# Joint grams of two block sizes, and one fixed order for three engines, in an RWKV-6 attention followed by an MLP mixer

## Chip, cores and metric

The kernel runs on one core of one Trainium2 chip. The metric is the device time of one execution in microseconds, from runs of the same program; the median is compared.

The engines are called by the names of the profile: PE (TensorE, the matrix unit), PEld (its weight loads), DVE (VectorE), ACT (ScalarE), POOL (GpSimd) and SP (SyncE, which here only issues DMAs).

## The reference

Two parts follow each other: a recurrent attention with a decay per channel, and a mixer over tokens and channels.

```python
B, H, S, D = 4, 8, 768, 48
for t in range(S):                      # attention, state is (B, H, D, D)
    cur = einsum('bhd,bhe->bhde', u * k[t], v[t])
    y[t] = einsum('bhd,bhde->bhe', r[t], state + cur)
    state = w[t][..., None] * state + einsum('bhd,bhe->bhde', k[t], v[t])
x = y as (B, S, H * D)                  # 384 channels
h = relu(x^T @ w_tok1) @ w_tok2         # tokens: 768 -> 256 -> 768
u = x + h^T
out = u + relu(u @ w_ch1) @ w_ch2       # channels: 384 -> 1536 -> 384
```

All arithmetic is in fp32. The mixer's weights arrive as 64-bit floats and are turned into fp32 by bit operations on VectorE.

## The kernel before

**Attention without a loop over tokens.** The 768 tokens of a batch are cut into three *units* of 256 tokens; there are twelve units, 0 to 11, and unit i belongs to batch i // 3. A unit holds two groups c of 128 tokens, and each of these two chunks of 64. Within a chunk the product of r and k with all decays between two tokens is built as a triangle of weights `at` (per head 64 by 64), and the outputs are `at` times v. Between chunks a state is carried.

The triangle is built by block doubling, in levels l = 0 to 5 with blocks of b = 2^l tokens. At a level, every right block of a pair of neighbours meets its left block: `gram(l)` multiplies k with the r of the right blocks on PE, `pick(l)` copies the wanted squares out of PSUM into `at` (through a mask with copy_predicated on DVE for levels 1 to 3, with four plain copies on ACT for level 4), and `join(l)` multiplies the decay of the neighbouring block into r and k on DVE, in place, so that the next level finds them relative to the bounds of a block twice as wide. `join(l)` changes what `gram(l)` reads, so it waits for it, and `gram(l+1)` waits for `join(l)`. Level 5 is `block(5)`: a gram with 32 weight columns, a join, and four copies on ACT. `begin` does the join of level 0.

[...] The heads have 48 channels, so these products use four tiles of the array, 64 rows by 64 columns each: `fours` issues one product to each of the four in turn. An fp32 product is two instructions on PE.

Units from `NEAR` = 6 on take the diagonal and level 0 from `nearest`: row sums on DVE of r times k for a token and its neighbour, loaded with tokens on partitions by `load_near` into tiles `kp` and `rp`, and then `place`, which puts them into `at`.

After its levels a unit goes through `post`: `tokens` transposes k, `carry` multiplies it with v for the state, `update` works the state on through four chunks on DVE, `before` multiplies r with the state of each chunk, and `within` adds `at` times v to it and copies the result to the mixer's input x on ACT.

**Mixer.** `mixing(bt)` gives lists of pieces for a batch: `hidden` (tokens in, 12 products), `back` and `turn` (tokens out and transposes), `up` (36 pieces, three pieces of 256 tokens by 12 blocks of hidden channels, with the result z taken out by ACT), and `quarters`: the last product by Strassen's seven half-size products p1 to p7 in Winograd's form, for which DVE makes four sums of z (`begin`: s1, s2, s4 and the new a21), and takes each product out of PSUM by an addition into the output o. Only the first piece of batch 0 uses the plain product (`down`).

**Order.** `woven` merges lists of pieces: every piece has a weight, and each list is spread evenly over the whole by weight. `emit` issues them in that order; a scheduler at build time may then move an instruction ahead of others on its engine. `strict` chains the instructions of PE and DVE one to the next, so that their order is the one written; before the change it is used only for the first three units. `beside(i, ...)` gives the pieces of unit i's post together with the levels of unit i + 1; `one` and `both` put the products of two pieces directly behind each other on PE.

The program runs as: units 0 to 2; then mixing 0 woven with units 3 to 5; mixing 1 with units 6 to 8; mixing 2 with units 9 to 11; mixing 3 alone.

**Buffers.** PSUM has two buffers of two banks for grams, transposes of k and (in batches 1 and 2) transposes of x (`ps_g`), one of two banks for state and outputs (`ps_a`), and two of one bank for the mixer's products (`ps_m`). The SBUF tiles named `rp` have two buffers, `kp` has one.

Of the kernel before, what the change touches and what calls it, by code (L numbers as in the profile page):

```python
# [10 lines left out]
f32 = mybir.dt.float32  # L11
bf16 = mybir.dt.bfloat16
u8 = mybir.dt.uint8
# [6 lines left out]
DM = H * D  # L20
T = 64
# [28 lines left out]
def emit(pieces):  # L50
    for _, f in pieces:
        f()
# [3 lines left out]
def rwkv6_then_mixer(  # L56
# [42 lines left out]
    def strict(*fs):  # L99

        for f in fs:
            done = len(block.instructions)
            f()
            for ins in block.instructions[done:]:
                if ins.engine in (pe.engine, dve.engine):
                    tc.add_manual_dep(ins, in_turn[ins.engine], no_sync, reason="order of issue")
                    in_turn[ins.engine] = ins.name

# [136 lines left out]
    def levels(i):  # L245
# [7 lines left out]
        def begin():  # L253
            decay = apool.tile([128, COLS // 2], f32, name="decay")
            L["w"] = apool.tile([128, UC, A, 2], f32, name="w_chunk", bufs=4)
            pool.memset(L["w"], 0.0)
            products.extend([w_, decay, w_[:, :COLS // 4], decay[:, :COLS // 8], w_[:, :COLS // 16],
                             decay[:, :COLS // 32], L["w"].rearrange("p c a j -> p (c a j)")])
            if i >= NEAR:
                join(0, products[0], products[1])  # L260
# [89 lines left out]
        def block(l):  # L350
            gram(l)
            join(l, products[l], products[l + 1])
            pick(l)

        L["steps"] = begin, gram0, pick0, gram, pick, lambda l: join(l, products[l], products[l + 1])
        pieces = [(0.1, begin)] + ([(1.6, first_block)] if i < NEAR else [])
        for l in range(1, LEVELS):
            pieces.append((1.2, lambda l=l: block(l)))
        return pieces

    def load_near(i):
        if i >= NU:
            return
        L = near_by[i] = [apool.tile([128, COLS], f32, name="kp", bufs=1)]
        for c in range(UC):
            t = apool.tile([128, COLS], f32, name="rp")
            sp.dma_start(t[:, :2 * DM].rearrange("p (two e) -> p two e", two=2), near[i - NEAR, c, :, :2, :])
            sp.dma_start(L[0][:, ts(c, DM)], near[i - NEAR, c, :, 2, :])
            L.append(t)

    def nearest(i):

        if not NEAR <= i < NU:
            return [(0.0, lambda: None)] * 2 + [(0.0, begin_near if i == NEAR - 1 else lambda: None)]
        sums = []

        def row(c):
            k, t = near_by[i][0][:, ts(c, DM)], near_by[i][1 + c]
            rr = t[:, :2 * DM].rearrange("p (two e) -> p two e", two=2)
            if c == 0:  # L380
                sums.append(apool.tile([128, UC, 2 * H], f32, name="sums"))
            dve.tensor_mul(rr, rr, k.unsqueeze(1).to_broadcast([128, 2, DM]))
            dve.tensor_mul(rr[:, 0], rr[:, 0], u_rows)
# [15 lines left out]


        return [(0.3, lambda c=c: late(newest(dve), dve, lambda: row(c))) for c in range(UC)] + [
            (0.2, lambda: (place(), load_near(i + 1)))]

    near_by = {}

    def begin_near():

        def parities():
# [3 lines left out]
        late(newest(dve), dve, parities)  # L412
        late(newest(sp), sp, lambda: sp.dma_start(u_rows, u_all))
        load_near(NEAR)

    def post(i):
        bt, half = divmod(i, UB)
# [23 lines left out]
                                      vt[ts(j, T), c, ts(2 * a + q, D)], start=True, stop=True)  # L441

        def update():
            L = live[i]
            kv = L.pop("kv")
            for c in range(UC):
                for j in range(2):
                    g = 2 * (half * UC + c) + j
                    if g == 2 * C - 1:
                        continue  # L450
                    new = apool.tile([128, A, D], f32, name="state", bufs=6)
                    got = kv[:, j, ds(c * A * D, A * D)].rearrange("p (a e) -> p a e", a=A)
                    if g == 0:
                        dve.tensor_copy(new, got)
                    else:
                        dve.tensor_mul(new, state[bt, g], L["w"][:, c, :, j].unsqueeze(2).to_broadcast([128, A, D]))
                        dve.tensor_add(new, new, got)  # L457
                    state[bt, g + 1] = new

# [24 lines left out]
        def within():  # L484
# [9 lines left out]
            for n in range(2):  # L494
                act.copy(x[ts(n, P), 1], got[ts(1 - n, P), 1])

        return [(1.0, tokens), (1.1, carry), (0.1, update), (1.1, before), (1.1, within),
                (0.01, lambda: load_rkw(i + 3)), (0.01, lambda: load_v(i + 3))]

# [19 lines left out]
    def mixing(bt):  # L519
# [51 lines left out]
        def quarters(s):  # L571
# [54 lines left out]
                dve.tensor_add(o[:, 0, HM:], o[:, 0, HM:], product(s4, w22))  # L626
                store(0)

            return [(0.01, begin)] + [(1.96, p) for p in (p1, p4, p2, p5, p6, p7, p3)]
# [11 lines left out]
    def beside(i, after, ahead):  # L641

        tokens, carry, update, before, within, *loads = after
        begin, *rest = ahead
        row0, row1, place = nearest(i + 1)
# [10 lines left out]
        return [(1.0, begin[1]), tokens, one(carry, rest[0]), update, one(before, rest[1]), one(within, rest[2]),  # L656
                *loads, *rest[3:], row0, row1, place]


    hiddens, turned, ups, downs = mixing(0)  # L660
# [8 lines left out]
    for steps in to_tok[:2]:  # L669
        steps[0]()  # L670
    (tok0, car0, upd0, bef0, wit0, *loads0), (tok1, car1, upd1, bef1, wit1, *loads1), (tok2, car2, upd2, bef2, wit2, *loads2) = (
        [f for _, f in post(i)] for i in range(3))
# [13 lines left out]
    for bt in range(B):  # L686
# [8 lines left out]
            pieces = downs[0][-4:] + [(0.01, weight_difference)] + downs[1] + ups[2] + downs[2]  # L695
        else:
            hiddens, pieces, ups, downs = mixing(bt)
            pieces = [(3.9, lambda h=h: emit(h)) for h in hiddens] + pieces
            for s in range(S // SEG):
                pieces += ups[s] + downs[s]  # L700
        n = (bt + 1) * UB
        if n < NU:
            att = []
            if bt == 0:

                begin, first, *rest = levels(n)
                att = [begin, (first[0], lambda f=first[1]: late(in_turn[dve.engine], dve, lambda: late(
                    in_turn[pe.engine], pe, f)))] + [(c, lambda f=f: late(converted, dve, f)) for c, f in rest]
            for i in range(n, n + UB):
                att += beside(i, post(i), levels(i + 1)) if i + 1 < NU else post(i)  # L710
            emit(woven(att, pieces))
        else:
            emit(pieces)

# [34 lines left out]
```

## Time and profile before

| what | us |
|---|---|
| median of 7 runs | 603.58 |
| lowest and highest | 602.91, 604.96 |
| the profiled execution, its own time | 603.58 |
| its span, first to last instruction | 601.9 |
| busy in the span: PE, PEld, DVE, ACT | 570.7, 487.5, 361.1, 177.5 |
| units 0 to 2 and first part of mixing 0 | 0 to 139.5 |
| mixing 0 with units 3 to 5 | 139.5 to 229 |
| mixing 1 with units 6 to 8 | 229 to 364 |
| mixing 2 with units 9 to 11 | 364 to 493 |
| mixing 3 | 493 to 601.9 |

In a row of the profile's groups, the line of the kernel is followed by engine, operation, output and inputs, shapes and count; behind the bar stand the busy time, the mean duration of one, and the idle time of the engine just before these instructions, with what ended it. A row of the timeline gives start and length of a stretch of equal instructions; matmuls overlap in the array, so what a stretch costs is read from its start to the start of the next. The granted clock of TensorE was full from 139.5 us on.

### The profile page before, as it was taken

The numbers are of one execution on the slowest core, as the hardware profiler recorded it, in microseconds if no ns is written. First come the engines' busy times: TensorE is split into PE (matmuls) and PEld (weight loads), VectorE is DVE, ScalarE is ACT, GpSimd is POOL, SyncE is SP. The second block draws the span as 40 slices with busy tenths as digits, with TensorE's granted clock in tenths as the row PEclk, the third lists the DMA queues.
The fourth block names the chain that finished last, engine by engine and source line by source line (L and its number), as shares of the span: only waits on it lengthen the run. The fifth ranks groups of instructions, "written<-read, shape, count | busy, mean of one in ns | idle before, by whom it ended". The sixth has DMA issues, their size and how long they took to land.

```text
span 601.9 us, 18874 instructions
## 1 busy us (share of the span) xinstructions
PE 570.7 (95%) x8596; PEld 487.5 (81%) x8596; DVE 361.1 (60%) x599; ACT 177.5 (29%) x428; POOL 7.2 (1%) x32
## 2 busy tenths in 40 slices
PE   2786999999999999999999999999999999999997
PEld 2776668866888886789989896789898986898987
DVE  5789699999775867666457366528446422040403
ACT  6154444422433313241141231231313312302020
POOL 4000000000000000000000000000000000000000
PEclk9997599999999999999999999999999999999999
DMA  8534555620334225141124113001200000000000
GB/s 331 204 83 152 162 171 177 211 70 19 91 105 111 69 82 158 30 132 29 53 57 132 28 28 106 2 2 35 74 2 28 2 27 0 1 19 8 27 2 27
DMA packets 22976, 45.85 MB, mean 76 GB/s; under 512 B 2512, under 2 KB 14928, under 8 KB 22896
## 3 DMA queue, kind: packets, MB, share of 16 engines
q1 hardware_dynamic: 22752, 44.64, 23.7%
q8 instruction: 67, 1.10, 0.8%
q14 instruction: 13, 0.11, 0.1%
q10 hardware_dynamic: 144, 0.00, 0.0%
HBM read 39.91 MB, written 4.72 MB: 74 GB/s over the span
## 4 chain that ended last, share of the span: by engine, by line
PE 81%; DVE 11%; issue 3%; DMA 2%; ACT 2%; SPq 0%; DVEq 0%; ACTq 0%
PE z_ps L554 26%; PE q_ps L588 24%; PE gram L307 7%; PE h_ps L527 6%; PE h_ps L534 4%; PE kv_ps L440 2%; PE y_ps L476 2%; PE y_ps L489 2%; DVE rk L341 2%; PE h_ps L564 2%; PE gram L430 2%; DVE at L323 1%; PE xT_ps L546 1%; PE gram L301 1%; DVE scratch L218 1%
## 5 line engine op out<-in xcount | busy, mean ns | idle before, releaser
L554 PE MATMUL z_ps<-xT,wch 128*128 128x256 f32 x864 | 195.6, 382 | 0.9 <-ACT z L556 0.9
L554 PEld LDWEIGHTS z_ps<-xT,wch 128*128 128x128 f32 x864 | 161.0, 190 | 22.8 <-ACT z L556 1.8
L556 ACT ACTIVATE z<-z_ps 128x256 f32<-128x256 f32 x144 | 55.1, 383 | 171.1 <-PE z_ps L554 158.2
L588 PE MATMUL q_ps<-wch,z 128*128 128x192 f32 x528 | 94.6, 329 | 0.0
L588 PEld LDWEIGHTS q_ps<-wch,z 128*128 128x128 f32 x528 | 86.1, 190 | 1.4
L588 PE MATMUL q_ps<-scratch,z 128*128 128x192 f32 x396 | 70.0, 328 | 0.0
L307 PE MATMUL gram<-rk 48*64 48x32 f32 x3072 | 62.7, 234 | 5.5 <-issue 2.3
L307 PEld LDWEIGHTS gram<-rk 48*64 48x64 f32 x3072 | 58.5, 153 | 11.1 <-issue 5.1
L341 DVE TENSOR_TENSOR rk<-rk,decay 112x1024 f32<-112x1024 f32 x36 | 44.0, 1223 | 36.7 <-PE gram L307 26.4
L588 PEld LDWEIGHTS q_ps<-scratch,z 128*128 128x128 f32 x396 | 64.5, 190 | 0.4
L341 DVE TENSOR_TENSOR rk<-rk,w 112x1024 f32<-112x1024 f32 x36 | 43.9, 1224 | 27.7 <-PE gram L307 22.0
L580 DVE TENSOR_TENSOR z<-z 128x768 f32<-128x768 f32 x11 | 10.5, 957 | 65.4 <-ACT z L556 65.4
L527 PE MATMUL h_ps<-x,wtok 128*128 128x384 f32 x96 | 35.9, 521 | 0.0
L534 PE MATMUL h_ps<-h,wtok 128*128 128x384 f32 x96 | 35.3, 492 | 0.0
L323 DVE COPY_PREDICATED at<-mask,gram 128x512 f32<-128x512 uint8 x36 | 32.3, 898 | 0.0
L457 DVE TENSOR_TENSOR state<-state,kv_ps 128x192 f32<-128x192 f32 x40 | 14.3, 356 | 24.6 <-PE kv_ps L440 23.8
L331 ACT COPY at<-gram 16x256 f32<-16x256 f32 x48 | 17.5, 364 | 33.6 <-PE gram L307 32.4
L536 DVE TENSOR_TENSOR x<-x,h_ps 128x384 f32<-128x384 f32 x24 | 13.3, 555 | 23.2 <-PE h_ps L534 23.1
L527 PEld LDWEIGHTS h_ps<-x,wtok 128*128 128x128 f32 x96 | 18.5, 201 | 10.4 <-issue 0.6
L534 PEld LDWEIGHTS h_ps<-h,wtok 128*128 128x128 f32 x96 | 16.5, 190 | 9.5 <-ACT h L529 2.6
L431 ACT COPY kT<-gram 128x512 f32<-128x512 f32 x24 | 14.1, 586 | 28.2 <-PE gram L430 28.1
L318 ACT COPY at<-gram 32x256 f32<-32x256 f32 x48 | 17.4, 364 | 14.4 <-PE gram L301 13.9
(84 smaller groups left out, 517.4 us busy)
## 6 DMA issues: line engine op xcount, KB each, us to landing
rk<-in_rkw_dram SPq DMA_DIRECT2D x36, 192.0 KB, 3.3
x<-in_w_ch_dram SPq DMA_DIRECT2D x10, 512.0 KB, 4.4
vt<-in_v_dram SPq DMA_DIRECT2D x12, 384.0 KB, 4.2
out_dram<-o SPq DMA_DIRECT2D x24, 192.0 KB, 1.9
rp<-in_near_dram SPq DMA_DIRECT2D x12, 384.0 KB, 3.6
scratch<-in_w_ch_dram SPq DMA_DIRECT2D x8, 512.0 KB, 4.1
w<-in_rkw_dram SPq DMA_DIRECT2D x18, 192.0 KB, 3.4
rk<-in_rkw_dram SPq DMA_DIRECT2D x6, 512.0 KB, 7.4
```

The source lines that it names most:

```text
L307: fours(lambda q, j, rows, cols: pe.matmul(g[cols, q, ts(ca, 32)], k_[rows, ds(ca * 128 + j * T, T)], right[rows, ts(2 * ca + j, 32 // b), ...
L318: act.copy(at[p:p + b, :, ts(c, A), b:], g[ds(p + c * b, b)])
L323: dve.copy_predicated(out=dst, data=g.rearrange("p q (m b) -> p q m b", b=b), mask=masks[l].rearrange("p x t -> p (x t)").rearrange("p (m ...
L331: act.copy(at[p:p + b, :, :, n * 2 * b + b:(n + 1) * 2 * b], g[p:p + b, :, :, ts(n, b)])
L341: dve.tensor_mul(halves, halves, by)
L431: act.copy(L["kT"][:, c], ps)
L457: dve.tensor_add(new, new, got)
L527: pe.matmul(sums[i], wtok1[:, c, ts(i, 128)], xs[bt][:, c, :], start=(c == 0), stop=(c == C - 1))
L534: pe.matmul(ps, wtok2[:, i, ts(c, 128)], h1[:, i, :], start=(i == 0), stop=(i == DTOK // 128 - 1))
L554: pe.matmul(ps, wch1[:, m, ts(jt, 128)], xT[:, m, ts(s, SEG)], start=(m == 0), stop=(m == DM // 128 - 1))
L556: act.activation(zs[s][:, jt, :], ps, AF.Relu)
L588: pe.matmul(ps, a[:, j, :], b[:, j, :], start=(j == 0), stop=(j == HJ - 1))
```

## The change

For units 6 to 11, the levels 1 and 2, and 3 and 4, are taken in one go. The block of four neighbours (quarters of b tokens) has six pairs. `spread` and `copies` write, for each group of 128 tokens, six blocks of r for every four (three of them with the decays of the quarters between multiplied in, on DVE, and three as copies on ACT) into a tile of the name `rp`. `gram4` multiplies k with them: 96 columns for every chunk instead of 32 in each of two levels. `pick4` copies the squares out with three copy_predicated for each group of tokens. `join_k` and `join_r` then multiply k and r by the decays of the block of four; `join_r` takes r's from the tile that spread filled. Level 5 stays. The masks for pick4 are made once in `begin_near`.

```diff
+        def spread(l, c):
...
+            dve.tensor_mul(y[:, :, 1:5:3], of[:, :, 2:4], by[:, :, 1:3].unsqueeze(3).to_broadcast([ROWS, G, 2, b]))
+            dve.tensor_mul(y[:, :, 2], y[:, :, 4], by[:, :, 1].unsqueeze(2).to_broadcast([ROWS, G, b]))
+        def copies(l):
...
+                act.copy(y[:, :, 0:4:3], r[:, ts(c, G), 1:3])
+                act.copy(y[:, :, 5], r[:, ts(c, G), 3])
+        def gram4(l):
+            for c in range(UC):
+                g = L["g", c] = ps_g.tile([128, 2, 512], f32, name="gram")
+                for a in range(A):
+                    fours(lambda q, j, rows, cols: pe.matmul(
+                        g[cols, q, ts(a, 96)], k_[rows, ds((c * A + a) * 128 + j * T, T)],
+                        L["far", c][rows, ts(2 * a + j, 96)], start=True, stop=True))
+        def join_k(l):
...
+            dve.tensor_mul(w[:, :, 2], w[:, :, 2], w[:, :, 3])
+            dve.tensor_mul(w[:, :, 1], w[:, :, 1], w[:, :, 2])
+            dve.tensor_mul(k[:, :, :3], k[:, :, :3], w[:, :, 1:].unsqueeze(3).to_broadcast([ROWS, UC * G, 3, b]))
+        def join_r(l):
...
+                dve.tensor_mul(r[:, ts(c, G), 1:].rearrange("p g q b -> p g (q b)"), y,
+                               w[:, ts(c, G), 0].unsqueeze(2).to_broadcast([ROWS, G, 3 * b]))
+            dve.tensor_mul(products[l + 2][:ROWS], w[:, :, 0], w[:, :, 1])
+        def pick4(l, c):
...
+            for q, first in enumerate((0, 3, 5)):
+                n = (3 - q) * b
+                dve.copy_predicated(out=to[:, :, :, (q + 1) * b:], data=got[:, :, :, first * b:first * b + n],
+                                    mask=masks4[l][:, q].unsqueeze(1).unsqueeze(3).to_broadcast([128, 2, A * 16 // b, n]))
```

`beside` writes a new order for the units 5 to 10. The row sums of a unit (`nearest`), which came at the end of the stretch before, now open its own stretch, in seven pieces; `update` is cut in two, and `load_near` for the next unit follows the second `join_r`. The three places where `both` puts products together are carry with the first joint gram, before with the second, and within with level 5. The weights of each unit's pieces are scaled to a sum of 12.

```diff
+        pieces = [*nearest(i), (0.3, tokens[1]), (1.9, begin[1]), far0, far1, (1.0, copies[1]), visit(carry, gram), join_k, join_r, loads[2],
+                  later0, pick0, loads[3], later1, copies_, pick1, visit(before, gram_), join_k_, join_r_, (0.01, lambda: load_near(i + 1)),
+                  pick0_, pick1_, visit(within, last), *loads[:2]]
+        total = sum(c for c, _ in pieces)
+        return [(c * 12 / total, f) for c, f in pieces]
```

Here `far` and `later` are spread for l = 1 and l = 3, a trailing underscore stands for l = 3, and loads[2] and loads[3] are the halves of update.

From mixing 1 to the end of mixing 2, `strict` now fixes the order, on ACT too. In the mixings 1 to 3 the four sums of `quarters` stand between the products, the products have weights of their own, and `hidden`, `back` and `turn` have smaller weights; `hidden` is emitted product by product.

```diff
-                if ins.engine in (pe.engine, dve.engine):
+                if ins.engine in in_turn:
...
+            return [(1.6, p1), (0.01, lambda: dve.tensor_add(s1, a21, a22)), (0.65, p4),
+                    (0.01, lambda: dve.tensor_sub(s2, s1, a11)), (0.65, p2), (0.01, lambda: dve.tensor_sub(a21, a11, a21)),
+                    (0.45, p5), (0.01, lambda: dve.tensor_sub(s4, a12, s2)), (0.3, p6), (1.0, p7), (1.6, p3)]
...
-            pieces = [(3.9, lambda h=h: emit(h)) for h in hiddens] + pieces
+            pieces = [(c * 0.5, f) for h in hiddens for c, f in h] + [(c * 0.3, f) for c, f in pieces]
...
-            emit(woven(att, pieces))
+            if bt == 0:
+                emit(woven(att, pieces))
+            else:
+                if bt == 1:
+                    in_turn = {e.engine: newest(e) for e in (pe, dve, act)}
+                strict(*(f for _, f in woven(att, pieces)))
```

More of the change, by code (lines that the diff above doesn't have):

```diff
@@ L259, in begin @@
             if i >= NEAR:
+                products[3], products[5] = w_[:, :COLS // 8], decay[:, :COLS // 32]
                 join(0, products[0], products[1])
@@ L353, in block, with fourths @@
             pick(l)
+        def fourths(l):
+            b = 1 << l
+            return (products[l].rearrange("p (g q) -> p g q", q=4)[:ROWS],
+                    *(t.rearrange("p (g q b) -> p g q b", q=4, b=b)[:ROWS] for t in (k_, r_)), COLS // (4 * b) // UC)
+        def spread(l, c):
+            b = 1 << l
+            w, _, r, G = fourths(l)
+            t = L["far", c] = apool.tile([128, COLS], f32, name="rp")
+            y = t[:, :COLS // UC * 3 // 2].rearrange("p (g s b) -> p g s b", s=6, b=b)[:ROWS]
+            of, by = r[:, ts(c, G)], w[:, ts(c, G)]
+            dve.tensor_mul(y[:, :, 1:5:3], of[:, :, 2:4], by[:, :, 1:3].unsqueeze(3).to_broadcast([ROWS, G, 2, b]))
+            dve.tensor_mul(y[:, :, 2], y[:, :, 4], by[:, :, 1].unsqueeze(2).to_broadcast([ROWS, G, b]))
@@ new lines, in copies @@
+        def copies(l):
+            b = 1 << l
+            _, _, r, G = fourths(l)
+            for c in range(UC):
+                y = L["far", c][:, :COLS // UC * 3 // 2].rearrange("p (g s b) -> p g s b", s=6, b=b)[:ROWS]
+                act.copy(y[:, :, 0:4:3], r[:, ts(c, G), 1:3])
+                act.copy(y[:, :, 5], r[:, ts(c, G), 3])
+        def gram4(l):
+            for c in range(UC):
+                g = L["g", c] = ps_g.tile([128, 2, 512], f32, name="gram")
[3 more added lines that the diff above has]
+                        L["far", c][rows, ts(2 * a + j, 96)], start=True, stop=True))
@@ new lines, in join_k @@
+        def join_k(l):
+            b = 1 << l
+            w, k, r, G = fourths(l)
+            dve.tensor_mul(w[:, :, 2], w[:, :, 2], w[:, :, 3])
+            dve.tensor_mul(w[:, :, 1], w[:, :, 1], w[:, :, 2])
+            dve.tensor_mul(k[:, :, :3], k[:, :, :3], w[:, :, 1:].unsqueeze(3).to_broadcast([ROWS, UC * G, 3, b]))
+        def join_r(l):
+            b = 1 << l
+            w, k, r, G = fourths(l)
+            for c in range(UC):
+                y = L.pop(("far", c))[:, :COLS // UC * 3 // 2].rearrange("p (g s b) -> p g (s b)", s=6, b=b)[:ROWS, :, :3 * b]
+                dve.tensor_mul(r[:, ts(c, G), 1:].rearrange("p g q b -> p g (q b)"), y,
+                               w[:, ts(c, G), 0].unsqueeze(2).to_broadcast([ROWS, G, 3 * b]))
+            dve.tensor_mul(products[l + 2][:ROWS], w[:, :, 0], w[:, :, 1])
@@ new lines, in pick4 @@
+        def pick4(l, c):
+            b = 1 << l
+            to = at_c[:, :, c].rearrange("p q a (m n) -> p q (a m) n", n=4 * b)
+            got = L.pop(("g", c))[:, :, :A * 96].rearrange("p q (m n) -> p q m n", n=6 * b)
+            for q, first in enumerate((0, 3, 5)):
+                n = (3 - q) * b
+                dve.copy_predicated(out=to[:, :, :, (q + 1) * b:], data=got[:, :, :, first * b:first * b + n],
+                                    mask=masks4[l][:, q].unsqueeze(1).unsqueeze(3).to_broadcast([128, 2, A * 16 // b, n]))
@@ L355, in levels @@
         L["steps"] = begin, gram0, pick0, gram, pick, lambda l: join(l, products[l], products[l + 1])
         pieces = [(0.1, begin)] + ([(1.6, first_block)] if i < NEAR else [])
+        if i >= NEAR:
+            return pieces + [(c, lambda f=f, a=a: f(*a)) for l in (1, 3) for c, f, a in (
+                (0.7, spread, (l, 0)), (0.7, spread, (l, 1)), (0.01, copies, (l,)), (0.3, gram4, (l,)), (1.7, join_k, (l,)),
+                (1.5, join_r, (l,)), (1.5, pick4, (l, 0)), (1.5, pick4, (l, 1)))] + [(1.4, lambda: block(5))]
@@ L361, in load_near @@
     def load_near(i):
-        if i >= NU:
-            return
         L = near_by[i] = [apool.tile([128, COLS], f32, name="kp", bufs=1)]
@@ L373, in nearest, with row @@
         if not NEAR <= i < NU:
-            return [(0.0, lambda: None)] * 2 + [(0.0, begin_near if i == NEAR - 1 else lambda: None)]
+            return []
         sums = []
-        def row(c):
+        def row(c, step):
             k, t = near_by[i][0][:, ts(c, DM)], near_by[i][1 + c]
             rr = t[:, :2 * DM].rearrange("p (two e) -> p two e", two=2)
[L380 to L383, printed above, removed]
+            if step == 0:
+                if c == 0:
+                    sums.append(apool.tile([128, UC, 2 * H], f32, name="sums"))
+                dve.tensor_mul(rr, rr, k.unsqueeze(1).to_broadcast([128, 2, DM]))
+                return
+            if step == 1:
+                dve.tensor_mul(rr[:, 0], rr[:, 0], u_rows)
+                return
             dve.tensor_reduce(out=sums[0][:, c], in_=t[:, :2 * DM].rearrange("p (h e) -> p h e", e=D),
@@ L398, in place, with quarters, masks @@
                 mask=masks[0].rearrange("p x (m two) -> p x m two", two=2).to_broadcast([128, 2 * UC * A, T // 2, 2]))
-        return [(0.3, lambda c=c: late(newest(dve), dve, lambda: row(c))) for c in range(UC)] + [
-            (0.2, lambda: (place(), load_near(i + 1)))]
+        return [(x, lambda c=c, n=n: late(newest(dve), dve, lambda: row(c, n)))
+                for c in range(UC) for n, x in enumerate((1.0, 0.6, 1.0))] + [(2.0, place)]
     near_by = {}
+    masks4 = {l: const.tile([128, 3, A * 16 >> l], u8, name=f"mask4_{l}") for l in (1, 3)}
     def begin_near():
+        def quarters(l, m):
+            b = 1 << l
+            n = 16 // b
+            pool.memset(m, 1.0)
+            for q in range(3):
+                for base, by in ((-q * b, 1), (q * b + b - 1, -1)):
+                    pool.affine_select(out=m[:, q], in_=m[:, q], compare_op=ALU.is_ge, fill=0.0, base=base,
+                                       pattern=[[-by * 4 * b, 2 * n]], channel_multiplier=by)
+            for j in range(2):
+                dve.tensor_copy(masks4[l][ts(j, T)].rearrange("p q (a n) -> p q a n", a=A),
+                                m[ts(j, T), :, ts(j, n)].unsqueeze(2).to_broadcast([T, 3, A, n]))
+        def masks():
+            t = apool.tile([128, COLS], f32, name="rp")
+            for l in masks4:
+                quarters(l, t[:, ts(l // 2, 48)].rearrange("p (q n) -> p q n", q=3)[:, :, :32 >> l])
         def parities():
@@ L410, in parities @@
             dve.tensor_scalar(odd, odd, -1.0, 1.0, op0=ALU.mult, op1=ALU.add)
-        late(newest(dve), dve, parities)
+        late(newest(dve), dve, lambda: (parities(), masks()))
         late(newest(sp), sp, lambda: sp.dma_start(u_rows, u_all))
-        load_near(NEAR)
     def post(i):
@@ L443, in update, with update_c @@
         def update():
+            for c in range(UC):
+                update_c(c)
+        def update_c(c):
             L = live[i]
[L445 to L458, printed above, removed]
+            kv = L["kv"] if c == 0 else L.pop("kv")
+            for j in range(2):
+                g = 2 * (half * UC + c) + j
+                if g == 2 * C - 1:
+                    continue
+                new = apool.tile([128, A, D], f32, name="state", bufs=6)
+                got = kv[:, j, ds(c * A * D, A * D)].rearrange("p (a e) -> p a e", a=A)
+                if g == 0:
+                    dve.tensor_copy(new, got)
+                else:
+                    dve.tensor_mul(new, state[bt, g], L["w"][:, c, :, j].unsqueeze(2).to_broadcast([128, A, D]))
+                    dve.tensor_add(new, new, got)
+                state[bt, g + 1] = new
         pairs = ((0, 0), (1, 0), (1, 1), (0, 1))
@@ L497, in post @@
         return [(1.0, tokens), (1.1, carry), (0.1, update), (1.1, before), (1.1, within),
-                (0.01, lambda: load_rkw(i + 3)), (0.01, lambda: load_v(i + 3))]
+                (0.01, lambda: load_rkw(i + 3)), (0.01, lambda: load_v(i + 3)),
+                *((1.4, lambda c=c: update_c(c)) for c in range(UC))]
     halves = [mpool.tile([128, NJ * SEG], f32, name=f"z{i}", bufs=1) for i in range(2)]
@@ L627, in p3 @@
                 store(0)
-            return [(0.01, begin)] + [(1.96, p) for p in (p1, p4, p2, p5, p6, p7, p3)]
+            if bt == 0:
+                return [(0.01, begin)] + [(1.96, p) for p in (p1, p4, p2, p5, p6, p7, p3)]
+            return [(1.6, p1), (0.01, lambda: dve.tensor_add(s1, a21, a22)), (0.65, p4),
+                    (0.01, lambda: dve.tensor_sub(s2, s1, a11)), (0.65, p2), (0.01, lambda: dve.tensor_sub(a21, a11, a21)),
+                    (0.45, p5), (0.01, lambda: dve.tensor_sub(s4, a12, s2)), (0.3, p6), (1.0, p7), (1.6, p3)]
         hiddens = [[(0.65, lambda i=i, c=c: hidden(i, c)) for c in range(C)] for i in range(DTOK // 128)]
@@ L644, in beside @@
         begin, *rest = ahead
-        row0, row1, place = nearest(i + 1)
         def both(f, g):
@@ L653, in one, with visit @@
             return (sum(c for c, _ in pieces), lambda: both(*(f for _, f in pieces)))
-        return [(1.0, begin[1]), tokens, one(carry, rest[0]), update, one(before, rest[1]), one(within, rest[2]),
-                *loads, *rest[3:], row0, row1, place]
+        if i + 1 < NEAR:
+            return [(1.0, begin[1]), tokens, one(carry, rest[0]), update, one(before, rest[1]), one(within, rest[2]),
+                    *loads[:2], *rest[3:], *([(0.0, begin_near)] if i == NEAR - 2 else [])]
+        far0, far1, copies, gram, join_k, join_r, pick0, pick1 = rest[:8]
+        later0, later1, copies_, gram_, join_k_, join_r_, pick0_, pick1_, last = rest[8:]
+        def visit(f, g):
+            return (0.3, lambda: both(f[1], g[1]))
+        pieces = [*nearest(i), (0.3, tokens[1]), (1.9, begin[1]), far0, far1, (1.0, copies[1]), visit(carry, gram), join_k, join_r, loads[2],
[3 more added lines that the diff above has]
+        return [(c * 12 / total, f) for c, f in pieces]
     hiddens, turned, ups, downs = mixing(0)
@@ L671, in rwkv6_then_mixer @@
     (tok0, car0, upd0, bef0, wit0, *loads0), (tok1, car1, upd1, bef1, wit1, *loads1), (tok2, car2, upd2, bef2, wit2, *loads2) = (
-        [f for _, f in post(i)] for i in range(3))
+        [f for _, f in post(i)[:7]] for i in range(3))
     levels(2)
@@ L709, in rwkv6_then_mixer @@
             for i in range(n, n + UB):
-                att += beside(i, post(i), levels(i + 1)) if i + 1 < NU else post(i)
-            emit(woven(att, pieces))
+                att += beside(i, post(i), levels(i + 1)) if i + 1 < NU else nearest(i) + post(i)[:7]
+            if bt == 0:
+                emit(woven(att, pieces))
+            else:
+                if bt == 1:
+                    in_turn = {e.engine: newest(e) for e in (pe, dve, act)}
+                strict(*(f for _, f in woven(att, pieces)))
         else:
```

## Prediction

> **What bounds the kernel now.** First the page's table of engines and its 40 slices, to find the engine that never rests:
>
> ```profile
> PE 570.7 (95%) x8596; PEld 487.5 (81%) x8596; DVE 361.1 (60%) x599; ACT 177.5 (29%) x428; POOL 7.2 (1%) x32
> PE   2786999999999999999999999999999999999997
> DVE  5789699999775867666457366528446422040403
> ```
>
> TensorE (PE) is full from the fifth slice on; VectorE (DVE) has holes. Next the stage windows: start to the first attention woven with mixing (0 to 139.5), the rest of that weave (to 229), mixing 1 with attention (to 364), mixing 2 with attention (to 500), mixing 3 alone:
>
> ```profile
> 139.50:229.00 89.50, 86.59 (x2294) 75.46 (x2294) 66.17 (x114) 29.55 (x77) 0.33 (x3) 1.00 0.29 82
> 229.00:364.00 135.00, 134.67 (x2065) 116.94 (x2064) 85.37 (x150) 36.70 (x92) 0.22 (x2) 1.00 0.24 72
> 364.00:500.00 136.00, 135.94 (x1764) 115.79 (x1763) 66.69 (x123) 33.03 (x82) 0.00 (x0) 1.00 0.10 30
> ```
>
> After span and colon: length, then busy time (and count) of PE, PEld, DVE, ACT, POOL. In mixings 1 and 2 PE is idle for 0.4 us of 271. So two things only can move the end here: PE work taken out, and PE waits put in. There are no waits to win.
>
> What PE work costs is read from its timeline, from start to start (matmuls are pipelined, so durations overlap):
>
> ```profile
> 302.62 1.10 PE L307 MATMUL gram<-rk 48*64 48x32 f32 x64
> 303.65 5.45 PE L554 MATMUL z_ps<-xT,wch 128*128 128x256 f32 x24
> 309.02 1.14 PE L307 MATMUL gram<-rk 48*64 48x32 f32 x64
> 310.09 2.22 PE L588 MATMUL q_ps<-wch,z 128*128 128x192 f32 x12
> 312.14 2.11 PE L588 MATMUL q_ps<-scratch,z 128*128 128x192 f32 x12
> 314.19 0.76 PE L301 MATMUL gram<-rk 48*32 48x32 f32 x64
> 314.87 2.22 PE L588 MATMUL q_ps<-wch,z 128*128 128x192 f32 x12
> ...
> 555.57 2.11 PE L588 MATMUL q_ps<-wch,z 128*128 128x192 f32 x12
> 557.52 2.11 PE L588 MATMUL q_ps<-scratch,z 128*128 128x192 f32 x12
> ```
>
> A gram of one level (64 instructions) takes 302.62 to 303.65 = **1.03 us**, 16.1 ns each. Twelve undisturbed products take 557.52 - 555.57 = 1.95 us, but 2.05 before a gram and 2.06 after one: each visit of the small grams among the large products costs about 0.1 + 0.1 = **0.2 us** beyond its own time.
>
> The prices for DVE come from the groups:
>
> ```profile
> L341 DVE TENSOR_TENSOR rk<-rk,decay 112x1024 f32<-112x1024 f32 x36 | 44.0, 1223 | 36.7 <-PE gram L307 26.4
> L323 DVE COPY_PREDICATED at<-mask,gram 128x512 f32<-128x512 uint8 x36 | 32.3, 898 | 0.0
> ```
>
> The second mixes two speeds: in the DVE timeline the level-1 pick, with runs of 2 elements, takes 1.30 us, levels 2 and 3, with runs of 4 and 8, take 0.70.
>
> [...] 64 level-5 products (32 weight columns) take 0.68 us, a gram with 64 weight columns 1.03.
>
> **The change, part by part.**
>
> *PE, the grams.* Units 6 to 11 each trade four grams (levels 1 to 4) for two joint ones, of 64 instructions with 96 moving columns. The large products give the column price: 72 of 256 columns took 15.54 us (540.03 to 555.57), 215.8 ns each, and those of 192 take 162.5, so 0.833 ns a column plus 2.5 ns. Alone, 96 columns take 82.5 ns; over four tiles 20.6. That four do overlap is shown for 64 columns: L284 had 64 of them in 1.06 us (185.09 to 186.15), 16.6 ns each against 55.8 alone, an overlap of 3.4. For 96 columns I take 20.6 ns, 1.32 us a gram; with the overlap of 3.4 it is 24.3 ns, 1.55 us; a cheaper one than 1.28 is excluded by the column price. Saving per unit: 4 x 1.03 - 2 x 1.32 = 1.48 us, times six = **8.9** (6.1 to 9.4).
>
> *PE, the visits.* Before, a unit made five (kv, y before and y within each with a gram, then levels 4 and 5 alone); now three (carry with the first gram, before with the second, within with level 5). 6 x 2 x 0.2 = **2.4** (1.2 to 3).
>
> *DVE.* Per unit it loses four 1.22 us joins, their small multiplies (0.42 + 0.29 + 0.22 + 0.19) and picks of 1.30 + 0.70 + 0.70: 8.7 us. It gains, for both joint levels: four spreads of 424 + 291 ns = 2.9; join_k 2 x 291 + 957 = 1.54 and 1.33; join_r 2 x 557 + 291 = 1.40 and 1.30; four picks of three copies (384, 256, 128 elements), at the trace's 1.1 ns an element (2.2 for runs of 2) plus 0.15 each about 1.35: 5.4. That is 13.9 us, 5.2 more per unit, 31 in all. It ends nothing while DVE keeps up, so it is priced as a wait below. The begin multiply, the row sums (7.0 us a unit) and the state updates are moved, not changed. The four quarter sums (0.95 each) go from ahead of p1 to between the products; none is needed before p5.
>
> *ACT.* Level-4 copies go (4 x 0.36), eight strided ones come (about 0.4 and 0.3 each, 2.6 us). ACT is 29% busy. In the fixed order z evacuations queue behind them; each needs only begin or join_r, which end over 1 us earlier on DVE. I cost this at nothing; without that cover it is up to 1.3 us a joint level.
>
> *SP, POOL.* load_near (four DMAs, landing in 3.6 and 3.8 us) waits for join_r of level 3, which frees the tiles. Row sums come at least 6 us of DVE work later, so no wait. load_rkw is issued after within, a unit ahead. The new masks cost 12 POOL selects of 0.45 us and two memsets once, under the first weave.
>
> *The fixed order.* I laid out the order that woven gives for mixings 1 and 2 and added up durations between the points where PE and DVE meet. Two stretches decide:
> - From the end of the first joint gram to the second half of the next, which needs the buffer freed by the second pick. DVE: 1.54 + 1.40 + 1.42 + 0.71 + 1.35 + 1.42 + 0.71 + 1.35 = 9.9 us. PE: seven "up" pieces of 1.295, the y products 0.97, half a gram 0.66, a visit 0.2: 10.9. Slack 1.0 in four of the five units; in the last of mixing 1 only six ups lie there: 9.6, a wait of 0.3.
> - From there to the next first gram. DVE: 1.33 + 1.30 + 2 x 1.35 + 1.40 + 7.0 + 1.9 + 1.42 = 17.1, and one quarter's sums and additions, 8.0: 25.1. PE: a quarter 13.65, seven ups 9.1, the rest 3.9: 26.7. Slack 1.6.
>
> So DVE is 93% loaded where it meets PE. Inside the six quarters a product waits when the one two before it isn't taken out (two buffers); attention pieces stand between the additions, and I find 0 to 0.5 us each. Sum of new waits: **2.5** (0.5 to 6). In the first weave, emitted as before, unit 6's share of the gains is counted and its 2.9 us of PE idle left as it is.
>
> **Sum:** 8.9 + 2.4 - 2.5 = 8.8 us. The profiled run had 603.58 us (span 601.9 and 1.7 around it), the median of seven exactly: 603.58 - 8.8 = **594.8**.
>
> **Rivals.**
> - *A: VectorE becomes the bound (slower).* Place: the picks and spreads between two joint grams. If all their short runs move at the level-1 pick's 2.2 ns an element, a pick is 2.2 us and a spread 1.15: each stretch grows by 2.6 us, past its slack by 1.6 (six times) and 1.0 (five times), 14.6 us, plus the 2.5: 603.6 - 11.3 + 17.1 = 609.4. It turns slower from 2.1 us more per stretch. For it: the 1.30 us pick, and 93%. Against: only the third copy at level 1 has runs of 2, and the multiplies over pairs (level-1 join) keep 1.22.
> - *B: most of the gain is eaten by waits.* Overlap of 3.4 and the upper wait, 6 us: 6.1 + 2.4 - 6 = 2.5, so 601.1. For it: one order for three engines has no give, the present one shows DVE idle some 40% beside a full PE. Against: the slacks above.
> - *C: the order costs nothing:* 603.6 - 11.3 = 592.3. For it: the stretches fit. [...]
> - *D: the joint grams are no shorter than the pairs they replace*, only visits go and waits come: 603.6, no change. It needs 2.06 us a gram, 32 ns an instruction, an overlap of 2.6; the 3.4 speaks against it.
>
> **Numbers.** The forecast 0.53, C 0.14, B 0.17, A 0.10, D 0.06. Faster by over 0.2% (1.2 us, about what a measurement of this kernel can tell from no change) are the forecast, C and most of B: 0.83; within: 0.07; slower: 0.10. The range goes from 591.3 (all ends good: 9.4 + 3 - 0.5 = 11.9 gained, and 0.4 for measuring) to 602.3, the edge of B.
>
> **What would show it.** Right: PE instructions down by 768; joint grams at 1.3 to 1.4 us start to start; three visits a unit; mixing 1 in some 129 to 131 us instead of 134.5; PE idle of 1 to 4 us in mixings 1 and 2, waiting for the second pick or for additions from q_ps. Wrong: joint grams above 1.6 us, picks above 1.7, or PE idle beyond 6 us there, on picks (A) or on z evacuations behind ACT's copies (B).

## The result

The changed kernel takes **600.8 us** in the median of 13 runs (599.36 to 601.86), against 603.91 for the kernel before (34 runs). The medians are 3.1 us apart, about a third of the 8.8 us that were forecast. The measured ratio, which is not the quotient of the two medians, is 0.9939 with a 95% interval of 0.9924 to 0.9953: faster by some 0.5%, and clear of no change. The profiled execution had 599.85 us, with a span of 597.8.

The page after has the same shape; these lines answer to those of before:

```profile
PE 562.2 (94%) x7828; PEld 480.9 (80%) x7828; DVE 391.7 (66%) x729; ACT 180.6 (30%) x452; POOL 9.6 (2%) x46
PE   3788899899999999999999999999999999999997
DVE  5789599999775795678778676668867142040413
```

TensorE has 768 instructions fewer, as worked out, and VectorE is busy for 30.6 us more, where 31 were forecast. The windows of the same two stretches show, beside VectorE's new work, one thing that was not there before:

```profile
229.00:364.00 135.00, 132.51 (x1686) 114.72 (x1685) 99.07 (x209) 37.46 (x102) 0.22 (x2) 1.00 0.24 73
364.00:500.00 136.00, 133.36 (x1508) 113.94 (x1507) 79.62 (x169) 34.22 (x90) 0.00 (x0) 1.00 0.08 27
```

Before, PE was idle for 0.4 us in these 271; now it is for 5.1. Its list of waits in mixing 1 (226 to 359 us) is short, total, count and longest in us:

```profile
PE gram L514 <- ACT kT L515: 2.1, 3, 0.7
PE xT_ps L634 <- DVE x L624: 0.4, 1, 0.4
```

Mixing 2 has the same two at 2.0 and 0.4, and 0.2 for a state. None is a wait for a pick or for an addition of the quarters (a partial product taken out of PSUM by VectorE), where the prediction had put them. L514 is a transpose of k in `tokens`, L515 the copy of it on ScalarE, L634 a transpose of x. In the timeline of PE after, one unit's visit to `tokens`, and its first joint gram:

```profile
282.72 1.46 PE L642 MATMUL z_ps<-xT,wch 128*128 128x256 f32 x6
284.01 0.60 PE L514 MATMUL gram<-ident,rk 128*128 128x128 f32 x4
285.29 0.66 PE L514 MATMUL gram<-ident,rk 128*128 128x128 f32 x4 [0.68 <-ACT kT L515]
285.78 4.05 PE L642 MATMUL z_ps<-xT,wch 128*128 128x256 f32 x18
289.76 1.15 PE L524 MATMUL kv_ps<-vt,kT 64*64 64x48 f32 x64
290.73 1.51 PE L386 MATMUL gram<-rp,rk 48*64 48x96 f32 x64
292.18 9.33 PE L642 MATMUL z_ps<-xT,wch 128*128 128x256 f32 x42
```

And the same visit in the timeline of the kernel before:

```profile
278.12 0.60 PE L430 MATMUL gram<-ident,rk 128*128 128x128 f32 x4
278.55 1.14 PE L588 MATMUL q_ps<-scratch,z 128*128 128x192 f32 x6
279.53 0.60 PE L430 MATMUL gram<-ident,rk 128*128 128x128 f32 x4
279.97 3.09 PE L588 MATMUL q_ps<-scratch,z 128*128 128x192 f32 x18
```

Four transposes take 0.43 us, and in both kernels the second four start only after ScalarE has copied the first. Before, the scheduler put three products of 192 columns (six instructions, 0.98 us) into that hole. In the fixed order both halves are one piece, and PE waits: 284.01 to 285.29 is 1.28 us instead of 0.43.

Adding the times from each start to the next gives TensorE's account of mixings 1 and 2 (the grams of units 7 to 11; those of unit 6 lie in the first weave). Large products are hidden, back, up and the quarters; kv and y are the products of carry, before and within:

| us in mixings 1 and 2 | before | after | difference | forecast |
|---|---|---|---|---|
| grams of levels 1 to 4 | 21.08 | 14.67 | -6.41 | -7.4 |
| large products, with the visits' cost | 212.75 | 210.47 | -2.28 | -2.0 |
| transposes of k | 5.27 | 10.67 | +5.40 | 0 |
| transposes of x | 4.19 | 5.16 | +0.97 | 0 |
| kv and both y products | 17.52 | 18.70 | +1.18 | 0 |
| level 5 | 3.43 | 3.41 | -0.02 | 0 |
| both mixings | 264.24 | 263.08 | -1.16 | -6.9, with 2.5 of waits |

By stage, from the first product of `hidden` of one mixing to that of the next (first weave: from its first gram):

| us | first weave | mixing 1 | mixing 2 |
|---|---|---|---|
| before | 89.40 | 134.57 | 129.67 |
| after | 87.26 | 133.03 | 130.05 |
| e1, two tiles | 86.55 | 130.67 | 127.73 |
| e2, split | 87.38 | 130.32 | 127.39 |
| e3, no fixed order | 87.19 | 135.17 | 127.33 |
| e4, before, fixed order | 89.56 | 145.73 | 138.40 |
| e5, split and turn moved | 87.67 | 129.73 | 126.79 |
| e6, split, no fixed order | 87.45 | 134.87 | 126.53 |

Mixing 2, where two units take the joint grams, got slower by 0.4 us. The first weave, still left to the scheduler, holds unit 6's share and got 2.1 us shorter, where 1.9 were forecast for a unit; the six profiles with this weave lie between 86.55 and 87.67, so that is its size and no more.

### The profile page after: what moved, and what is told of

It is laid out like the page before. It is cut to its first block, busy times and chain, and to the rows that moved or that the text cites. A ratio compares the mean times of both kernels' runs of the same rounds, so it can differ in the third digit from the quotient of the medians.

```text
span 597.8 us, 17493 instructions
## 1 busy us (share of the span) xinstructions
PE 562.2 (94%) x7828; PEld 480.9 (80%) x7828; DVE 391.7 (66%) x729; ACT 180.6 (30%) x452; POOL 9.6 (2%) x46
## 4 chain that ended last, share of the span: by engine, by line
PE 80%; DVE 11%; DMA 3%; ACT 3%; issue 3%; SPq 0%; DVEq 0%; ACTq 0%
PE z_ps L642 29%; PE q_ps L676 24%; PE h_ps L622 5%; PE h_ps L615 4%; PE gram L308 4%; PE gram L386 3%; DMA x<-in_w_ch_dram 2%; PE y_ps L576 2%; PE kv_ps L524 2%; PE h_ps L652 2%; DVE rk L342 2%; PE y_ps L563 2%; PE gram L514 2%; PE xT_ps L634 1%; PE gram L302 1%
## 5 line engine op out<-in xcount | busy, mean ns | idle before, releaser
L308 PEld LDWEIGHTS gram<-rk 48*64 48x64 f32 x1536 | 33.4, 172 | 8.5 <-issue 3.4
L308 PE MATMUL gram<-rk 48*64 48x32 f32 x1536 | 35.7, 251 | 4.6 <-issue 1.9
L720 DVE TENSOR_TENSOR z<-z 128x768 f32<-128x768 f32 x9 | 8.6, 954 | 47.4 <-ACT z L644 47.4
L342 DVE TENSOR_TENSOR rk<-rk,decay 112x1024 f32<-112x1024 f32 x24 | 29.4, 1224 | 13.5 <-PE gram L302 7.7
L412 DVE COPY_PREDICATED at<-mask,gram 128x384 f32<-128x384 uint8 (+2 forms) x72 | 34.5, 482 | 1.4
L615 PE MATMUL h_ps<-x,wtok 128*128 128x384 f32 x96 | 34.0, 507 | 0.0
L342 DVE TENSOR_TENSOR rk<-rk,w 112x1024 f32<-112x1024 f32 x24 | 29.3, 1223 | 5.2 <-PE gram L308 4.9
L514 PE MATMUL gram<-ident,rk 128*128 128x128 f32 x96 | 17.0, 305 | 8.1 <-ACT kT L515 6.9
L580 ACT COPY x<-y_ps 128x384 f32<-128x384 f32 x12 | 5.7, 479 | 59.0 <-PE y_ps L576 59.0
L686 DVE TENSOR_TENSOR o<-x,z 128x192 f32<-128x192 f32 x11 | 3.9, 356 | 27.2 <-ACT z L685 27.1
```

Of the source, the lines that this page charges most:

```text
L308: fours(lambda q, j, rows, cols: pe.matmul(g[cols, q, ts(ca, 32)], k_[rows, ds(ca * 128 + j * T, T)], right[rows, ts(2 * ca + j, 32 // b), ...
L342: dve.tensor_mul(halves, halves, by)
L412: dve.copy_predicated(out=to[:, :, :, (q + 1) * b:], data=got[:, :, :, first * b:first * b + n], mask=masks4[l][:, q].unsqueeze(1).unsquee ...
L514: pe.transpose(ps[:, a, :], k_[:, ts(c * A + a, 128)], ident)
L615: pe.matmul(sums[i], wtok1[:, c, ts(i, 128)], xs[bt][:, c, :], start=(c == 0), stop=(c == C - 1))
```

## The experiments

**e1: the two halves in two PSUM tiles.** What makes the second half wait is taken away, in the same order.

```diff
-            both = ps_g.tile([128, 2, 512], f32, name="gram").rearrange(...)
             for c in range(UC):
-                ps = both[:, c]
+                ps = ps_g.tile([128, 2, 512], f32, name="gram").rearrange(...)[:, 0]
```

Expected: 

> The changed kernel, but the two halves of k's transposes go into two PSUM tiles instead of the two banks of one; same order. Theory W (the fixed order leaves nothing between the halves, and the second waits for ScalarE's copy of the first because they share a tile): tokens fall from 1.79 us a unit to about 0.9 in the two mixings under the fixed order, TensorE's waits on kT there from 4.1 us to under 0.5, and the time by 4 to 5 us against the changed kernel, to about 596. Rival X (the wait is not due to the shared tile but to ScalarE or the order of issue): no change, 600.8, waits as they were.

Measured: 597.03 us, ratio to the kernel before 0.9878 (0.9838 to 0.9917). The waits of PE in the two mixings (225 to 484 us) are

```profile
PE xT_ps L633 <- DVE x L623: 0.8, 2, 0.4
PE y_ps L562 <- DVE state L543: 0.2, 1, 0.2
```

The wait on kT (2.1 and 2.0 us after the change) is gone, and the mixings are 2.4 and 2.3 us shorter than after the change. So the second half waited because it shares a tile with the first, though it writes the tile's other half. Rival X of this run falls.

**e2: the hole filled instead.** One tile, but two pieces (loads[4] and loads[5], the last two of post), with `place` and so some mixing between. The lines that split `tokens` are not shown.

```diff
...
-        pieces = [*nearest(i), (0.3, tokens[1]), (1.9, begin[1]),
+        *rows, put = nearest(i) or [(0.0, lambda: None)]
+        pieces = [*rows, (0.15, loads[4][1]), put, (0.15, loads[5][1]), (1.9, begin[1]),
...
-                att += ... else nearest(i) + post(i)[:7]
+                att += ... else nearest(i) + post(i)[-2:] + post(i)[1:7]
```

Expected: 

> The changed kernel, one shared tile as there, but the second half of k's transposes is a piece of its own, with place and some mixing between the halves. W: the wait is covered by mixing products, so again 4 to 5 us less than the changed kernel, about 596, and both halves cost 0.44 us each from start to start. X (the loss is in the sum of TensorE's work or in VectorE, not in this wait): within 1 us of 600.8.

Measured: 596.0 us, ratio 0.9858 (0.9821 to 0.9895), 4.8 us below the changed kernel. Transposes of k cost 2.61 and 2.62 us in the two mixings, 0.44 a half, as before the change. In the timeline large products stand in the hole again:

```profile
285.44 0.60 PE L518 MATMUL gram<-ident,rk 128*128 128x128 f32 x4
285.88 1.46 PE L646 MATMUL z_ps<-xT,wch 128*128 128x256 f32 x6
287.18 0.60 PE L518 MATMUL gram<-ident,rk 128*128 128x128 f32 x4
```

Waits left:

```profile
PE xT_ps L638 <- DVE x L628: 0.8, 2, 0.4
PE y_ps L567 <- DVE state L548: 0.2, 1, 0.2
```

Two ways of removing one wait give about the same, and rival X falls here too.

**e3: the changed kernel without the fixed order.**

```diff
-            if bt == 0:
-                emit(woven(att, pieces))
-            else:
...
-                strict(*(f for _, f in woven(att, pieces)))
+            emit(woven(att, pieces))
```

Expected: 

> The changed kernel with all its pieces and weights, but mixings 1 and 2 issued as before the change, so that the scheduler may move instructions. W: the scheduler puts products between the halves of the transposes, as it did in the kernel before; the 4.1 us of waits go and the time is 596 to 598. Rival Y (the fixed order is what makes the joint grams pay; the scheduler moves them badly, with waits elsewhere): slower than the changed kernel, 602 to 605, with TensorE waits on VectorE.

Measured: 600.42 us, ratio 0.9931 (0.9908 to 0.9953): the same as with the fixed order, but only because two differences cancel. Mixing 1 is 2.1 us longer and mixing 2 is 2.7 us shorter than after the change. My theory had 596 to 598, rival Y 602 to 605, and it is neither. The theory was right on its wait and incomplete on the rest. PE's waits in mixing 1:

```profile
PE q_ps L676 <- DVE o L690: 3.0, 2, 1.6
PE h_ps L615 <- ACT x L582: 1.3, 1, 1.3
PE gram L514 <- ACT kT L515: 0.2, 1, 0.2
```

The scheduler fills the hole in `tokens` (0.2 us left of 2.1), but a quarter product now waits twice for an addition on VectorE that frees its buffer, and hidden waits for ScalarE's copy of the last unit. The first of these is a wait I had forecast for the fixed order; it appears without it.

**e4: the fixed order alone, on the kernel before.**

```diff
-                if ins.engine in (pe.engine, dve.engine):
+                if ins.engine in in_turn:
...
-            emit(woven(att, pieces))
+            if bt == 0:
+                emit(woven(att, pieces))
+            else:
...
+                strict(*(f for _, f in woven(att, pieces)))
```

Expected: 

> The kernel before, grams and pieces as they were, with the fixed order on TensorE, VectorE and ScalarE for mixings 1 and 2 alone. W: each of six units gets the wait between the halves of its transposes (0.9 us) and the two mixings the wait before the last transpose of x (0.4 us): 6 us more than before, about 610, possibly more where block's gram, join and pick stand close together. X: the fixed order costs nothing, about 604.

Measured: 623.02 us, ratio 1.0322 (1.0279 to 1.0364), 19 us slower. In the mixings (228 to 513 us) PE waits for

```profile
PE gram L430 <- ACT kT L431: 4.3, 6, 0.7
PE q_ps L588 <- DVE o L602: 3.5, 1, 3.5
PE z_ps L554 <- DVE z L620: 2.5, 1, 2.5
PE xT_ps L546 <- DVE x L536: 2.5, 3, 1.8
PE q_ps L588 <- DVE o L610: 1.9, 1, 1.9
PE y_ps L476 <- DVE state L457: 0.8, 1, 0.8
PE z_ps L554 <- ACT z L556: 0.5, 1, 0.5
```

The hole of 0.7 us is there six times, as forecast. But 6 us were expected and 19 came; the waits above make 16.0 of them. A fixed order is therefore not cheap by itself: in the pieces and weights of the kernel before it cost 19 us, in those of the changed kernel it costs nothing in sum (600.8 us, and 600.42 without it). Which of the new pieces and weights makes the difference was not tested.

**e5: the other wait, with e2.** The last transpose of x moves behind the first up piece.

```diff
+            last_turn = pieces.pop()
+            ups[0].insert(1, last_turn)
```

Expected: 

> The kernel with the split transposes of k (e2), and the last transpose of x in mixings 1 to 3 one up piece later, so that it doesn't stand directly behind the sum it waits for. W: the two waits of 0.4 us for that sum go, xT falls from 2.56 to about 2.1 us in each of the two mixings, and the time by about 0.8 to 1 us against e2, to about 595. Rival: the wait moves to the next piece that needs the buffer; no change against e2, 596.

Measured: **595.43 us**, ratio 0.9858 (0.9837 to 0.9880), the fastest median of all kernels here. Its own runs of the kernel before had a median of 603.1, so it is 7.7 us below it. Each mixing is 0.6 us shorter than e2's, and the waits of PE in both are one line:

```profile
PE y_ps L567 <- DVE state L548: 0.2, 1, 0.2
```

The medians of e2 and e5 come from different chips, and their intervals overlap; the step between them is shown by the stages and the list of waits, not by the medians. The rival, that the wait only moves to another piece, falls.

**e6: the split, without the fixed order.** The edit is that of e3 on e2.

Expected: 

> The kernel with the split transposes of k (e2), without the fixed order in mixings 1 and 2. Theory F (once its hole is filled, the fixed order is worth something by itself, as it keeps the additions that free the product buffers in time): 599 to 601, as without the split, with TensorE waits of 3 to 5 us on the quarter additions and on ScalarE's copies. Rival: the fixed order is worth nothing beyond the pieces and weights: 596, the same as e2.

Measured: 599.56 us, ratio 0.9936 (0.9915 to 0.9957), as theory F had it. With its hole filled, the fixed order brings 4.5 us in mixing 1 (130.32 against 134.87), whose waits here are

```profile
PE q_ps L680 <- DVE o L694: 3.1, 2, 1.7
PE h_ps L619 <- ACT x L586: 1.3, 1, 1.3
```

and costs 0.9 us in mixing 2 (127.39 against 126.53).

**e7: every joint gram issued twice.** On e2, to find why a joint gram takes 1.45 to 1.48 us and not 1.32. It does redundant work and nothing else.

```diff
-                for a in range(A):
+                for a in [*range(A), *range(A)]:
```

Expected: 

> The kernel with the split transposes of k (e2), with the products of every joint gram issued twice into the same place. It measures the joint gram. Theory T (streaming as priced, 20 to 20.6 ns a product, and a fixed tail of 0.1 to 0.2 us before the next large product): the joint gram goes from 1.46 to between 2.74 and 2.78 us from start to start. Rival R (a lower overlap of the four tiles, 22.7 ns for every product): 2.9 us.

Measured (one run, 617.97 us), in the timeline of PE:

```profile
255.09 1.15 PE L528 MATMUL kv_ps<-vt,kT 64*64 64x48 f32 x64
256.17 2.87 PE L386 MATMUL gram<-rp,rk 48*64 48x96 f32 x128
258.97 9.33 PE L646 MATMUL z_ps<-xT,wch 128*128 128x256 f32 x42
```

And the single one at this place in e2:

```profile
252.70 1.55 PE L386 MATMUL gram<-rp,rk 48*64 48x96 f32 x64
254.18 9.33 PE L646 MATMUL z_ps<-xT,wch 128*128 128x256 f32 x42
```

The doubled gram takes 2.80 us from start to start, just above theory T's 2.74 to 2.78; the single one took 1.48. So 64 more instructions cost 1.32 us, 20.6 ns each: the rate was priced exactly, and 0.16 us does not grow with their number. Rival R, 2.9 us for every doubled gram, is out. Five of the ten doubled grams in the two mixings run through like this one. In four others PE pauses between two instructions for 0.24 to 0.58 us without a releaser in the profile, so their times say nothing of the rate.

## Why the prediction was wrong

**The bound** was right. TensorE still fills the span of mixings 1 and 2 (busy for 258 of 263 us), and what came or went is seen on it.

**The grams**: right in mechanism, with one term missing. Streaming was priced at 1.32 us, and e7 confirms its 20.6 ns. The fixed 0.16 us of a joint gram was not in the sum. The level grams' 1.03 us, read from start to start, held whatever is fixed in them; the 1.32 was worked out from the column rate alone. The prediction's own line for L284 showed the term: 64 products of 64 columns at a quarter of 55.8 ns are 0.89 us, and they took 1.06. The 0.17 left over was read as an overlap of 3.4 instead of four. The ten joint grams took 1.47 us on average, 1.5 us more than priced in sum; the level grams took 1.05 instead of 1.03, which gives 0.5 back. So about 1 us of the 7.4 was missing.

**The visits** fit: 2.28 us against 2.0, read from the large products as a whole and not visit by visit.

**VectorE**: its work was priced too low, though the two stretches held. The prices of the multiplies, 957 ns for 768 elements and 557, 424 and 291 ns for 384, 256 and 128, agree with what such multiplies take in the groups and the DVE timeline of before:

```profile
L580 DVE TENSOR_TENSOR z<-z 128x768 f32<-128x768 f32 x11 | 10.5, 957 | 65.4 <-ACT z L556 65.4
L383 DVE TENSOR_TENSOR rp<-rp,u_rows 128x384 f32<-128x384 f32 x12 | 6.7, 555 | 0.2
273.12 0.42 DVE L342 TENSOR_TENSOR w<-decay 112x256 f32<-112x256 f32 x1
289.43 0.29 DVE L342 TENSOR_TENSOR decay<-w 112x128 f32<-112x128 f32 x1
```

The 0.15 us for every copy of a pick was an estimate; the multiplies of 768 and 384 elements above, 957 and 555 ns, leave 0.153 us that does not grow with the elements. The page counts time in which two instructions overlap only once, and gives 30.6 us more. Adding the durations of the instructions, as the prediction did, gives 36.2 more instead of 31: picks cost 1.65 us at l = 1 and 1.38 at l = 3, against 1.35, and the small multiplies of join_k at l = 1 took 0.39 and 0.41, against 0.29. So 30.6 against 31 is luck. In the fixed order PE did not wait for a pick or a quarter addition once. The only wait for a pick, 0.87 us, is unit 6's, outside that order. Rival A had no part in it.

**ScalarE and GpSimd**: the strided copies, put at about 0.4 and 0.3 us, took 417 and 307 ns in the mean, and the 12 selects, put at 0.45 us, took 0.26 and 0.19.

**The fixed order is the step that failed:** its term of 2.5 us of new waits (0.5 to 6) left out the waits inside a piece. I wrote that I "added up durations between the points where PE and DVE meet". That is one pair of engines. PE and ScalarE meet inside `tokens`, where PE needs ScalarE's copy to go on. The prediction named ScalarE only for z and for the copies at the levels, and put nothing for this wait. The timeline of the kernel before showed it: in mixings 1 and 2 the two halves never stand together, and in the first three units, whose order was fixed already, PE waits for it three times:

```profile
PE gram L430 <- ACT kT L431: 3.0, 3, 1.1
```

The scheduler had hidden all of it in the two mixings; the fixed order paid about 0.7 us of idle time in each of six units. Measured, +5.4 us on the transposes of k from start to start, 4.1 of it idle; e2 gives back 5.4 and e1 4.7. The same slip, smaller, stands at the last transpose of x: it comes directly behind the sum that it needs (+0.97 us in both mixings together, which e5 gives back). The remaining +1.18 on kv and y has two parts. About half is gone in e3 and e6, so it goes with the fixed order of the new pieces (e4, with the old ones, does not show it); why is open. The rest stays in all kernels with the new pieces: y followed by level 5 takes 1.08 us from start to start where y followed by a gram with 64 weight columns takes 0.97. The cause of these 0.11 us was not shown.

So the rows of the transposes and of kv and y grew together by 7.55 us in mixings 1 and 2, where 2.5 of waits were forecast in all. PE's idle time, 5.1 us, is only a part of it, and none of it lay where I had looked. With both holes closed, e5 has these mixings in 256.5 us, 6.6 less than the changed kernel, where 5.7 of the forecast 6.9 were missing.

Rival B's 601.1 us came near the time. Its size of the waits (6 us) and its reason, that one order has no give, fit; its place, z evacuations behind ACT's copies, does not, and e7 contradicts its overlap of 3.4. Its closeness is part luck. Rival C, an order that costs nothing, is refuted by the idle 5.1 us, and rival D with 1.47 us against 2.06 for the pair of levels.

## What to carry to other kernels

When an order that a scheduler made is replaced by a written one, list for every piece the dependencies inside it, on every engine, and ask what used to stand in the gap: a wait of 0.7 us in each of six pieces ate more than half of what the shorter products had brought. A piece in which one engine hands to another and gets the work back should be cut there, or given a second buffer; either was worth some 4 to 5 us here (600.8 us against 597.03 and 596.0). And price work on a full engine from start to start, with the part that does not grow with the number of instructions as a term of its own (0.16 us of the 1.48 of a joint gram here).

## What the runs showed of the hardware

A joint gram of 32 fp32 products stands in the profile as 64 instructions on PE. With 96 moving columns in four tiles of 64 rows by 64 columns, they took 20.6 ns each in e7. That is a quarter of the 82.5 ns that one would take alone by the prediction's estimate from the large products (215.8 ns with 256 columns, 162.5 with 192), so by this estimate the four overlap fully. Join_k's multiplies of 128 elements, which take every fourth element, took 0.39 and 0.41 us in the mean, where spread's of the same size took 0.29 (289 and 294 ns), as expected. And the first stretch of the kernel, which no edit here touches, ended anywhere between 138.7 and 143.7 us in the profiled executions, while mixing 3 took TensorE 105.4 us in all nine. That is why the stages, and not the spans, are compared above.
